# A table of 18 sets of scheduling allowances by stretch of 16 units, and attention copies from PSUM that go to ScalarE or VectorE

## The chip, the cores and the metric

One core of one Trainium2 chip. The metric is the device time of one launch in microseconds. A core has TensorE for matmuls (PE in the profile; PEld is its loading of weights), VectorE (DVE), ScalarE (ACT), GpSimd (POOL) and SyncE (SP), which here issues all DMAs. Each engine works through its own queue in order. An instruction that must wait for another engine holds up everything behind it in its own queue.

## The reference, cut to what matters

```
h   = mab(inducing, x)                    # 32 inducing points attend to 12480 tokens, 4 batches
out = mab(x, h)                           # each token attends to the 32 rows of h
# mab(q, kv): s = q @ kv.T / sqrt(128); a = softmax(s); a @ kv
x = out.reshape(49920, 128)
h = x @ w_in                              # 128 -> 2048
P = a0 + a1*h + a2*h**2 + a3*h**3
Q = 1 + |b0|*|h| + |b1|*h**2
out = (P / (Q + 1e-6)) @ w_out            # 2048 -> 128
```

## The kernel before, in words

The kernel computes a first layer and a second one around a rational function of 2048 hidden values per token. The tokens stand in 104 tiles of 480 (4 batches of 26), the hidden values in 8 groups of 256. A tile with a group is a **unit** (`b_n_q` in the names), 832 in all, 128 partitions by 960 numbers each.

A unit goes through these steps. PE multiplies into a PSUM bank pair, `h` (`first`, L964): the rows of `st` are `w_in` already multiplied by the 32 rows of `h` of that batch, so the token's softmax weights `at` are the moving operand. Of two units, the even one ("masked") gets its absolute value on DVE (`u<-h`, int32) or, when DVE is late, on ACT (event `taken`), then a shift on POOL (`pre`, `l<-u,all`) and its numerator on DVE (`D`, `l<-h,all,l`). The odd one gets its absolute value on ACT (`abs`, `u<-h,all`) and `D` (`l<-u,all,h`) on DVE. `D` frees the bank. ACT then takes the logarithm of two units at once (`ln`, `u<-u,all`, 1920 wide), and later a sigmoid, in one of three forms: into a PSUM bank for one unit (`sigp`, `i<-u`), after which DVE finishes (`Ev`, `l<-l,all,i`), or in SBUF for one unit or two (`sig`, `sig2`, `u<-u`, 960 or 1920 wide), after which POOL finishes in two instructions (`add`, `l<-l,all`, and `Eg`, `l<-l,u`). Logarithm and sigmoid need different tables, so ACT works in rounds: a table load, some logarithms, a table load, some sigmoids. There are 3 bank pairs for `h` and `i` together. Last, PE adds the unit to its tile's output, `po` (`second`, L974), DVE copies a full output to `oT` (`fetch`, L991), and SP stores it.

Beside the units run two chains of attention work, as Python generators that yield what they need next. `ahead` (L934) prepares the next batch: scores `pc`, their softmax `e`, the transpose `pt` and its copy to SBUF `eT` (`score`, L606), the weighted sum `ph` (`weigh`), then `HT`, the four pieces `pg` of `st` with their copies `gs` (`piece`, L756; two copies of 256 columns each, then a cast and a subtraction in `split`), and the linear part with `pgt` and its copy `gt` (`linear`, L802). `attend` (L948) makes the softmax weights of four tiles at a time: `pd`, `a`, a transpose `pa`, its copy `hl` (`quotients`, L878), the rest of that number on DVE into the other half of `hl`, and 16 DMAs `at<-hl` that spread it over four tiles. There is one buffer `hl`, so the next copy waits for these DMAs. All these matmul results share one PSUM bank (`misc`).

What order all this stands in is not written by hand. Class `Flow` (L188) plans the whole program ahead, while it is built. It keeps a clock per engine, a cost for every event (`COST`), and takes at each step the event that can start first. Between events of one engine that could start within the allowance `WAIT` it takes the one with the smallest sum of ready time and `RANK` (for attention work `GEN`). `LOAD` and `FULL` say how a backlog of DVE or POOL shifts the choice among the three forms of sigmoid. In the kernel before these numbers hold for the whole program. The order is then pinned: every instruction carries the semaphores it needs, and nothing is decided at run time. Which engine a copy stands on is written in the generators:

```
yield "a", 0.56                                     # eT (L643), hl (L898): ScalarE
nc.scalar.activation(eT[:, :, rows], pt[0:TP, :, rows], AF.Identity, bias=0.0, scale=1.0)
yield "v", 0.5                                      # gs (L777): VectorE, once per half
nc.vector.tensor_scalar(out=g[:, h], in0=pg[:, h], scalar1=self.scale, scalar2=None, op0=ALU.mult)
```

`gt` (L815) is on ScalarE too. Until `Flow` starts (the first 94 us, `self.boot`), the order is that of the Python program.

Of the kernel before, what the change touches and what calls it, by code (L numbers as in the profile page):

```python
# [187 lines left out]
class Flow:  # L188
# [167 lines left out]
    def do(self, what, u, start, end):  # L356
# [44 lines left out]
        elif what == "again":  # L401
            k.first(u, True)
            u.t["d"], u.moved = end + 0.1 + LAT, True
            self.pres.remove(u)
            self.ds.append(u)
# [89 lines left out]
class Kernel:  # L495
# [260 lines left out]
    def piece(self, b, j):  # L756

        nc = self.nc
        extra = j == self.F // 512
# [5 lines left out]
        if extra:  # L765
            for i, q in enumerate(qs):
                nc.tensor.matmul(pg[:, 2 * P * i:2 * P * i + 2 * P], self.HT[b], self.w_in[:, 2 * P * q:2 * P * q + 2 * P], start=True, stop=True)
        else:
            nc.tensor.matmul(pg, self.HT[b], self.w_in[:, 512 * j:512 * j + 512], start=True, stop=True)
# [382 lines left out]
```

## Time and profile before

| | |
|---|---|
| runs | 2318.00, 2318.13, 2320.06 us (median 2318.13) |
| the profiled execution | 2318.69 us, of which the span from the first to the last instruction is 2316.9 |
| granted TensorE clock, mean | 0.975 of full |
| busy, of the span | PE 2111.2, DVE 2053.4, ACT 2162.6, POOL 2009.5 us |
| units' matmuls begin | 92.98 us |
| last instruction of ACT, of DVE | begin at 2298.57 (four sigmoids, 3.65 us) and 2311.28 us |

Busy times of engines overlap, so they don't add up to the span. A row of a table by group gives the line (L165 for everything, since one helper records all instructions), engine, operation, output and inputs by the program's names, shape, count, then busy time and mean time of one, then the time for which the engine stood idle before these instructions and who ended it. A row of waits says which group of an engine waited for which of another, the sum in us, how often, and the longest.

### The profile page before, as it was taken

The page shows a single profiled execution, that of the slowest core. Times are in us where ns is not written, and L with a number is a line of the kernel's source. Part 1 is how long each engine was busy: PE and PEld are TensorE (multiplying, and loading weights), DVE is VectorE, ACT ScalarE, POOL GpSimd, SP SyncE. Part 2 cuts the span into 40 slices and gives each one's busy share as a digit, 9 for nine tenths or more (in the row PEclk, how much of TensorE's full clock was granted, in tenths as well). Part 3 has the DMA queues.
Part 4 walks back from the last instruction along what each step waited for, and adds up shares of the span by engine and source line. Part 5 has one row for each costly group of instructions (what it writes and reads, how often), then busy time and mean ns, then how long its engine had stood idle before and what let it go on. Part 6 is the DMA issues. An engine that isn't in the chain of part 4 may idle for free.

```text
span 2316.9 us, 24295 instructions
## 1 busy us (share of the span) xinstructions
PE 2111.2 (91%) x7744; PEld 1160.7 (50%) x7744; DVE 2053.4 (89%) x2204; ACT 2162.6 (93%) x1824; POOL 2009.5 (87%) x1425
## 2 busy tenths in 40 slices
PE   5689999899999999998998999999899998899888
PEld 3455555444555545454554555454455554454443
DVE  5688999989999998999999899898999998988895
ACT  1389999999999999999999999999999999999997
POOL 1269987999999896999998989999989999998995
PEclk7589999999999999999999999999999999999999
DMA  9222322211022221220121223221110111011000
GB/s 277 56 64 62 93 78 60 60 43 43 22 74 59 77 69 60 77 69 24 36 60 52 65 72 94 60 69 35 43 43 19 42 43 43 26 43 35 17 26 19
DMA packets 78639, 133.70 MB, mean 58 GB/s; under 512 B 13544, under 2 KB 63976, under 8 KB 78504
## 3 DMA queue, kind: packets, MB, share of 16 engines
q1 hardware_dynamic: 78504, 132.06, 19.4%
q8 instruction: 65, 1.06, 0.2%
q14 instruction: 70, 0.57, 0.1%
HBM read 80.89 MB, written 25.56 MB: 46 GB/s over the span
## 4 chain that ended last, share of the span: by engine, by line
ACT 25%; POOL 23%; PE 23%; DVE 16%; issue 8%; DMA 1%; SPq 1%; ACTq 0%; POOLq 0%; DVEq 0%
POOL l L165 23%; ACT u L165 18%; PE po L165 15%; DVE l L165 10%; ACT i L165 4%; PE h L165 4%; DVE u L165 3%; ACT L165 2%; PE ph L165 2%; SPq L165 1%; PE pd L165 1%; DMA at<-hl 1%; DVE oT L165 1%; DMA xT<-x_c 1%; PE pgt L165 0%
## 5 line engine op out<-in xcount | busy, mean ns | idle before, releaser
L165 PE MATMUL po<-l,w_out 128*128 128x480 f32 x3328 | 1472.1, 576 | 72.2 <-DVE oT L165 40.6
L165 POOL TENSOR_TENSOR l<-l,u 128x960 f32<-128x960 f32 x458 | 1026.7, 2242 | 37.7 <-ACT u L165 12.8
L165 PEld LDWEIGHTS po<-l,w_out 128*128 128x128 f32 x3328 | 614.7, 191 | 601.9 <-issue 457.5
L165 ACT ACTIVATE u<-u,all 128x1920 f32<-128x1920 f32 x416 | 774.3, 1892 | 4.8 <-DVE l L165 4.3
L165 PE MATMUL h<-at,st 128*128 128x480 f32 x1664 | 647.6, 482 | 81.8 <-DVE l L165 73.3
L165 POOL TENSOR_SCALAR l<-u,all 128x960 f32<-128x960 f32 x416 | 444.7, 1070 | 148.8 <-DVE u L165 121.3
L165 DVE SCALAR_TENSOR_TENSOR l<-u,all,h 128x960 f32<-128x960 f32 x416 | 501.0, 1207 | 57.4 <-ACT u L165 56.3
L165 DVE SCALAR_TENSOR_TENSOR l<-h,all,l 128x960 f32<-128x960 f32 x416 | 500.9, 1211 | 50.6 <-POOL l L165 47.8
L165 DVE TENSOR_SCALAR u<-h 128x960 int32<-128x960 int32 x400 | 457.7, 1149 | 44.2 <-PE h L165 37.1
L165 POOL TENSOR_SCALAR l<-l,all 128x960 f32<-128x960 f32 x458 | 491.0, 1072 | 1.5
L165 PEld LDWEIGHTS h<-at,st 128*128 128x128 f32 x1664 | 295.5, 192 | 384.1 <-issue 193.9
L165 DVE SCALAR_TENSOR_TENSOR l<-l,all,i 128x960 f32<-128x960 f32 x374 | 442.8, 1207 | 39.1 <-ACT i L165 38.1
L165 ACT ACTIVATE u<-h,all 128x960 f32<-128x960 f32 x416 | 435.8, 1050 | 19.8 <-PE h L165 16.2
L165 ACT ACTIVATE u<-u 128x960 f32<-128x960 f32 (+1 forms) x300 | 417.9, 1415 | 0.2
L165 ACT ACTIVATE i<-u 128x960 f32<-128x960 f32 x374 | 354.8, 965 | 16.4 <-DVE l L165 14.3
L165 ACT ACT_TABLE_LOAD x148 | 189.9, 1283 | 3.3 <-PEq L1145 0.7
L165 PEld LDWEIGHTS pd<-HT,xT 128*120 128x120 f32 x832 | 106.8, 192 | 25.1 <-issue 16.6
L165 PE MATMUL pd<-HT,xT 128*120 128x32 f32 x832 | 101.2, 267 | 5.2 <-issue 3.8
L165 PE MATMUL po<-at,st 128*128 128x480 f32 x104 | 78.1, 751 | 1.6 <-POOL st L165 1.6
L165 DVE COPY oT<-po 128x480 f32<-128x480 f32 x104 | 67.3, 647 | 12.7 <-PE po L165 12.7
L165 POOL TENSOR_TENSOR cv<-cv 128x384 f32<-128x384 f32 (+2 forms) x11 | 12.2, 1114 | 67.4 <-DVE cv L165 53.4
L165 ACT ACTIVATE e<-pc,nm 128x480 f32<-128x480 f32 (+1 forms) x28 | 18.4, 657 | 50.3 <-DVE nm L165 47.2
(96 smaller groups left out, 707.2 us busy)
## 6 DMA issues: line engine op xcount, KB each, us to landing
xT<-x_c SPq DMA_DIRECT2D x182, 240.0 KB, 3.2
x<-x_t SPq DMA_DIRECT2D x104, 240.0 KB, 4.2
at<-hl SPq DMA_DIRECT2D x416, 60.0 KB, 2.0
out<-oT SPq DMA_DIRECT2D x104, 240.0 KB, 2.2
xTw<-x_c SPq DMA_DIRECT2D x5, 960.0 KB, 10.8
raw<-w_in SPq DMA_DIRECT2D x4, 480.0 KB, 9.4
raw<-w_out SPq DMA_DIRECT2D x5, 384.0 KB, 9.7
xTw<-x_c SPq DMA_DIRECT2D x2, 480.0 KB, 8.7
```

The costliest lines, as they stand in the source:

```text
L165: ins = call(*args, **kw)
```

## The change

Three things change. The planner's numbers become 18 sets (`SETS`), of which each stretch of 16 units takes one (`PLAN`, 52 entries): before each step, `plan` looks at how many units have been added to an output and loads the set of that stretch into `RANK`, `GEN`, `WAIT`, `LOAD` and `FULL`. The copies `eT`, `gs`, `gt` and the first half of `hl` ask for "either", and the planner offers them on ScalarE with the rank `GEN["ac"]` and on VectorE with `GEN["vc"]`; the new function `copy` writes the instruction for whichever engine was taken. And a path that no unit took before (`EXTRA`, `again`) is removed; `MASKED` may differ by batch but is the same for all four. What a unit computes does not change.

```diff
-    GEN = {"pe": 110.4, "v": 80.9, "a": 9.2, "g": 75.8, "x": -14.3}
+    GEN = {"pe": 110.4, "v": 80.9, "a": 9.2, "ac": 9.2, "vc": 30.0, "g": 75.8, "x": -14.3}
+    SPAN = 16
+    KEYS = ("RANK.first", "RANK.second", "RANK.fetch", "RANK.D", "RANK.mask", "RANK.Ev", "RANK.abs", "RANK.ln", "RANK.wide", "RANK.one", "RANK.sig", "RANK.pre", "RANK.add", "RANK.Eg", "RANK.load", "RANK.take", "GEN.pe", "GEN.v", "GEN.a", "GEN.ac", "GEN.vc", "GEN.g", "GEN.x", "WAIT.pe", "WAIT.v", "WAIT.a", "WAIT.g", "LOAD.v", "LOAD.g", "FULL",)
+    SETS = (
+        (-52.7, 123.6, -33.4, 11.7, -22, 1.8, -15.1, 19.8, 56.7, 28.7, -167.4, 11.5, 86.9, 76.3, 9.6, 38, 110.4, 80.9, 9.2, 9.2, 30, 75.8, -14.3, 0.1, 0.06, 0, 0.26, -0.17, -1.05, 15),
...
+        (-51.1, 123.6, -33.4, 11.7, -22, 1.3, -15.1, 19.8, 57.9, 28.7, -155.4, 11.5, 92.3, 106.7, 9.6, 38.7, 110.4, 80.9, -7.4, 9.2, 41.8, 75.8, -12.3, 0.1, 0.06, 0, 0.2, -0.17, -1.05, 16.5),
...
+    )
+    PLAN = (16, 6, 17, 10, 7, 12, 0, 13, 0, 4, 17, 5, 9, 4, 11, 17, 6, 12, 12, 0, 3, 6, 2, 13, 11, 8, 17, 11, 6, 6, 3, 15, 14, 13, 4, 16, 6, 16, 17, 3, 12, 5, 16, 0, 2, 1, 14, 14, 4, 14, 0, 0)
...
+    def plan(self):
+        n = min(self.i2 // self.SPAN, len(self.PLAN) - 1)
+        if n == self.stretch:
+            return
+        self.stretch = n
+        for key, value in zip(self.KEYS, self.SETS[self.PLAN[n]]):
+            name, _, kind = key.partition(".")
+            if kind:
+                getattr(self, name)[kind] = value
+            else:
+                setattr(self, name, value)
...
+            elif kind == "either":
+                for engine in ("a", "v"):
+                    yield engine, t.ready, self.GEN[engine + "c"], cost, ("turn", t)
...
             ways = {}
+            self.plan()
...
+            self.by = engine
...
+    def copy(self, out, in_, scale=1.0, shift=0.0):
+        if self.flow is None or self.flow.by == "a":
+            self.nc.scalar.activation(out, in_, AF.Identity, bias=shift, scale=scale)
+        elif isinstance(scale, float) and isinstance(shift, float):
+            self.nc.vector.tensor_copy(out=out, in_=in_)
+        else:
+            self.nc.vector.tensor_scalar(out=out, in0=in_, scalar1=scale, scalar2=shift, op0=ALU.mult, op1=ALU.add)
...
-        yield "a", 0.56
-        nc.scalar.activation(eT[:, :, rows], pt[0:TP, :, rows], AF.Identity, bias=0.0, scale=1.0)
+        yield "either", 0.56
+        self.copy(eT[:, :, rows], pt[0:TP, :, rows])
...
-            moved = extra or self.shifted(q)
-            if self.boot:
-                nc.scalar.activation(g[:, h], pg[:, h], AF.Identity, bias=self.params.k2 if moved else 0.0, scale=self.scale)
-                continue
-            yield "v", 0.5
-            if moved:
-                nc.vector.tensor_scalar(out=g[:, h], in0=pg[:, h], scalar1=self.scale, scalar2=self.params.k2, op0=ALU.mult, op1=ALU.add)
-            else:
-                nc.vector.tensor_scalar(out=g[:, h], in0=pg[:, h], scalar1=self.scale, scalar2=None, op0=ALU.mult)
+            yield "either", 0.45
+            self.copy(g[:, h], pg[:, h], self.scale, self.params.k2 if self.shifted(b, q) else 0.0)
...
-        yield "a", 0.56
-        nc.scalar.activation(gt, pt[:, 0:self.NF], AF.Identity, bias=self.params.lin_shift, scale=self.params.lin_scale)
+        yield "either", 0.6
+        self.copy(gt, pt[:, 0:self.NF], self.params.lin_scale, self.params.lin_shift)
...
-        yield "a", 0.56
-        nc.scalar.activation(hl[rows, 0], pt[rows, 0:BT], AF.Identity, bias=0.0, scale=1.0)
+        yield "either", 0.56
+        self.copy(hl[rows, 0], pt[rows, 0:BT])
```

Where the orders differ, at three places. In the names `po0_0` is the output of batch 0, tile 0; `l0_0_4` unit 4 of that tile; `h0_1_0` the first product of the next tile; the last number is a buffer's.

**The start, PE's queue.** Batch 1 begins with the scores `pc1_0`, while tile 0 is still being added up. Before:

```order
L165 MATMUL po0_0_0_823<-l0_0_2_765,w_out_93 128x480 x2
L165 MATMUL po0_0_0_823<-l0_0_3_778,w_out_93 128x480 x2
L165 MATMUL pa0_1_907<-ident_76,a0_1_752 96x120 x4
L165 MATMUL po0_0_0_823<-l0_0_4_812,w_out_93 128x480 x2
L165 MATMUL po0_0_0_823<-l0_0_5_818,w_out_93 128x480 x2
L165 MATMUL pc1_0_936<-xT1_0_888,ind_74 32x480
L165 MATMUL pc1_0_936<-xT1_1_890,ind_74 32x480
L165 MATMUL pc1_0_936<-xT1_2_892,ind_74 32x480
L165 MATMUL pc1_0_936<-xT1_3_894,ind_74 32x480
L165 MATMUL h0_1_0_956<-at0_1_0_921,st_0_700 128x480 x2
```

Now:

```order
L165 MATMUL po0_0_0_828<-l0_0_2_765,w_out_93 128x480 x2
L165 MATMUL pa0_1_900<-ident_76,a0_1_752 96x120 x4
L165 MATMUL po0_0_0_828<-l0_0_3_785,w_out_93 128x480 x2
L165 MATMUL pc1_0_929<-xT1_0_869,ind_74 32x480
L165 MATMUL pc1_0_929<-xT1_1_871,ind_74 32x480
L165 MATMUL pc1_0_929<-xT1_2_873,ind_74 32x480
L165 MATMUL pc1_0_929<-xT1_3_875,ind_74 32x480
L165 MATMUL po0_0_0_828<-l0_0_4_808,w_out_93 128x480 x2
L165 MATMUL h0_1_0_953<-at0_1_0_913,st_0_700 128x480 x2
```

The scores have moved ahead of the last two pairs of tile 0's output that stood before them, and the transpose `pa0_1`, whose copy feeds tile 1, stands directly behind one pair of `po0_0` instead of two.

**The copy `hl` of batch 3, tiles 4 to 7.** On ACT before (its other half follows on DVE):

```order
L165 ACTIVATE u3_2_0_11900<-u3_2_0_11900,all_94 128x1920
L165 ACTIVATE u3_2_2_11921<-h3_2_3_11934,all_94 128x960
L165 ACT_TABLE_LOAD
L165 ACTIVATE i3_0_6_11972<-u3_0_6_11712 128x2x480
L165 ACTIVATE hl3_4_11961<-pa3_4_11956 128x480
L165 ACTIVATE i3_0_7_11979<-u3_0_6_11712 128x2x480
L165 ACTIVATE i3_1_0_11985<-u3_1_0_11737 128x2x480
```

On DVE now, with the first half as a `CAST`, and the second half as before:

```order
L165 COPY oT2_25_11956<-po2_25_0_11815 128x480
L165 TENSOR_SCALAR u3_2_4_11944<-h3_2_4_11946 128x960
L165 SCALAR_TENSOR_TENSOR l3_2_3_11921<-u3_2_2_11908,all_94,h3_2_3_11922 128x960
L165 CAST hl3_4_11955<-pa3_4_11950 128x480
L165 SCALAR_TENSOR_TENSOR l3_0_6_11711<-l3_0_6_11711,all_94,i3_0_6_11966 128x960
L165 SCALAR_TENSOR_TENSOR l3_0_7_11735<-l3_0_7_11735,all_94,i3_0_7_11972 128x960
L165 SCALAR_TENSOR_TENSOR l3_2_4_11945<-h3_2_4_11946,all_94,l3_2_4_11945 128x960
L165 TENSOR_TENSOR hl3_4_11955<-pa3_4_11950,hl3_4_11955 128x480
```

ACT's queue no longer holds this copy; DVE's now holds it, with two `Ev` (`l3_0_6`, `l3_0_7`) and one `D` between it and its second half. Counted over the program, 14 of 29 `hl`, 14 of 28 `eT` and 2 of 4 `gt` go from ACT to DVE, and 18 of 28 `gs` go from DVE to ACT. Among the units, 369 instead of 374 sigmoids go to PSUM (and so to DVE's `Ev`), 463 instead of 458 units are finished on POOL, 161 instead of 158 sigmoids are two units wide and 141 instead of 142 one unit wide in SBUF, and ACT takes the absolute value of 20 instead of 16 masked units. In the first 104 units POOL finishes 64 instead of 55, of them 6 instead of 3 in tile 0. The table loads are 148 in both, and PE's and SP's instructions are the same in number and kind.

**The end, PE's queue**, from the last but one product `h3_25_6` on. Before:

```order
L165 MATMUL h3_25_6_14714<-at3_24_1_14558,st_3_11207 128x480 x2
L165 MATMUL po3_23_0_14687<-l3_23_2_14434,w_out_93 128x480 x2
L165 MATMUL po3_23_0_14687<-l3_23_3_14455,w_out_93 128x480 x2
L165 MATMUL po3_23_0_14687<-l3_23_6_14488,w_out_93 128x480 x2
L165 MATMUL h3_25_7_14740<-at3_24_1_14558,st_3_11207 128x480 x2
L165 MATMUL po3_23_0_14687<-l3_23_5_14476,w_out_93 128x480 x2
L165 MATMUL po3_23_0_14687<-l3_23_7_14498,w_out_93 128x480 x2
L165 MATMUL po3_23_0_14687<-at3_20_3_14326,st_3_11207 128x480
L165 MATMUL po3_24_0_14759<-l3_24_0_14508,w_out_93 128x480 x2
L165 MATMUL po3_24_0_14759<-l3_24_2_14546,w_out_93 128x480 x2
```

Now:

```order
L165 MATMUL po3_23_0_14659<-l3_23_6_14485,w_out_93 128x480 x2
L165 MATMUL h3_25_5_14721<-at3_24_1_14542,st_3_11257 128x480 x2
L165 MATMUL po3_23_0_14659<-l3_23_7_14510,w_out_93 128x480 x2
L165 MATMUL po3_23_0_14659<-at3_20_3_14332,st_3_11257 128x480
L165 MATMUL h3_25_6_14735<-at3_24_1_14542,st_3_11257 128x480 x2
L165 MATMUL h3_25_7_14744<-at3_24_1_14542,st_3_11257 128x480 x2
L165 MATMUL po3_24_0_14749<-l3_24_0_14533,w_out_93 128x480 x2
L165 MATMUL po3_24_0_14749<-l3_24_1_14552,w_out_93 128x480 x2
L165 MATMUL po3_24_0_14749<-l3_24_4_14585,w_out_93 128x480 x2
```

The additions to output 23 that stood behind the last product `h3_25_7` (`l3_23_5`, `l3_23_7` and the linear part `at3_20_3`) now stand ahead of the last two. On DVE the copy of output 23, which stood behind the `D` of `l3_25_7`, now stands ahead of it. Outputs 24 and 25 follow in both.

## Rows read from the trace of the kernel before

**Rows 1.** The page, busy time, share of the span and instructions of each engine

```profile
PE 2111.2 (91%) x7744; PEld 1160.7 (50%) x7744; DVE 2053.4 (89%) x2204; ACT 2162.6 (93%) x1824; POOL 2009.5 (87%) x1425
```

**Rows 2.** The page, chain that ended last, shares by engine

```profile
ACT 25%; POOL 23%; PE 23%; DVE 16%; issue 8%; DMA 1%; SPq 1%; ACTq 0%; POOLq 0%; DVEq 0%
```

**Rows 3.** Windows: length, then busy us (instructions) of PE, PEld, DVE, ACT, POOL, clock

```profile
84.00:136.00 52.00, 42.26 (x158) 26.33 (x159) 32.99 (x42) 32.90 (x35) 15.78 (x14) 0.74 0.19 49
136.00:385.00 249.00, 233.98 (x951) 133.43 (x951) 229.45 (x232) 246.40 (x212) 219.19 (x158) 0.96 0.25 72
136.00:2302.00 2166.00, 2009.57 (x7208) 1098.88 (x7208) 1971.89 (x1962) 2117.83 (x1766) 1980.84 (x1394) 0.99 0.18 52
```

**Rows 4.** ACT's waits from 136 to 2302 us: sum, times, longest

```profile
ACT i L165 <- DVE l L165: 14.3, 26, 1.9
...
ACT u L165 <- PE h L165: 13.1, 20, 2.2
...
ACT hl L165 <- DMA at<-hl: 7.3, 6, 1.8
...
ACT hl L165 <- DMA x<-x_t: 1.7, 2, 1.3
...
ACT hl L165 <- PE h L165: 1.3, 1, 1.3
```

**Rows 5.** Timeline of ACT: two `hl` that waited for DMAs

```profile
315.93 0.57 ACT L165 ACTIVATE hl<-pa 128x480 fp32r<-128x480 f32 x1 [0.45 <-DMA x<-x_t]
...
1797.95 0.57 ACT L165 ACTIVATE hl<-pa 128x480 fp32r<-128x480 f32 x1 [1.26 <-DMA at<-hl]
```

**Rows 6.** ACT by group and shape: busy us, mean ns, idle before

```profile
L165 ACT ACTIVATE eT<-pt 120x512 f32<-120x512 f32 x24 | 14.3, 594 | 7.4 <-PE pt L165 7.4
...
L165 ACT ACTIVATE hl<-pa 128x480 fp32r<-128x480 f32 x23 | 13.0, 565 | 8.7 <-DMA at<-hl 6.8 <-DMA x<-x_t 1.7
...
L165 ACT ACTIVATE gs<-pg,all 128x256 f32<-128x256 f32 x4 | 1.9, 516 | 1.8 <-PE pg L165 1.8
...
L165 ACT ACTIVATE i<-u 128x960 f32<-128x960 f32 x374 | 354.8, 965 | 16.4 <-DVE l L165 14.3 <-PE po L165 0.7 <-PE h L165 0.2
...
L165 ACT ACTIVATE u<-h 128x960 f32<-128x960 f32 x16 | 15.4, 962 | 3.3 <-PE h L165 3.3
...
L165 ACT ACTIVATE u<-u 128x1920 f32<-128x1920 f32 x158 | 281.9, 1796 | 0.2
```

**Rows 7.** DVE by group and shape

```profile
L165 DVE COPY oT<-po 128x480 f32<-128x480 f32 x104 | 67.3, 647 | 12.7 <-PE po L165 12.7
...
L165 DVE TENSOR_SCALAR gs<-pg,all 128x256 f32<-128x256 f32 x28 | 13.6, 498 | 0.1
...
L165 DVE SCALAR_TENSOR_TENSOR l<-l,all,i 128x960 f32<-128x960 f32 x374 | 442.8, 1207 | 39.1 <-ACT i L165 38.1
...
L165 DVE TENSOR_SCALAR u<-h 128x960 int32<-128x960 int32 x400 | 457.7, 1149 | 44.2 <-PE h L165 37.1 <-POOL l L165 6.2
```

**Rows 8.** POOL by group and shape

```profile
L165 POOL TENSOR_TENSOR l<-l,u 128x960 f32<-128x960 f32 x458 | 1026.7, 2242 | 37.7 <-ACT u L165 12.8
...
L165 POOL TENSOR_SCALAR l<-l,all 128x960 f32<-128x960 f32 x458 | 491.0, 1072 | 1.5
```

**Rows 9.** ACT's waits from 84 to 136 us

```profile
ACT e L165 <- DVE nm L165: 4.5, 1, 4.5
```

**Rows 10.** The chain that ended last, 84 to 140 us: start, length, what

```profile
124.40 3.23 PE po L165 x8
```

**Rows 11.** Timeline of the end: start, length, group, idle before, releaser

```profile
2298.57 3.65 ACT L165 ACTIVATE i<-u 128x960 f32<-128x960 f32 x4
...
2299.57 4.59 DVE L165 SCALAR_TENSOR_TENSOR l<-l,all,i 128x960 f32<-128x960 f32 x4 [1.75 <-ACT i L165]
...
2283.77 13.15 PE L165 MATMUL po<-l,w_out 128*128 128x480 f32 x32 [1.70 <-DVE oT L165]
...
2297.88 13.15 PE L165 MATMUL po<-l,w_out 128*128 128x480 f32 x32 [0.75 <-DVE oT L165]
```

More of the change, by code (lines that the diff above doesn't have):

```diff
@@ L191 @@
     LAT = 0.15
-    COST = {"first": 0.56, "second": 1.60, "linear": 0.35, "again": 0.6, "fetch": 0.6, "D": 1.13, "mask": 1.08, "Ev": 1.13, "abs": 0.95, "ln": 1.79, "sig": 1.70, "half": 0.90, "load": 1.4, "pre": 1.06, "add": 1.11, "Eg": 2.22}
-    RANK = {"again": 40, "first": -52.7, "second": 123.6, "fetch": -33.4, "D": 11.7, "mask": -22, "Ev": 1.8, "abs": -15.1, "ln": 19.8, "wide": 56.7, "one": 28.7, "sig": -167.4, "pre": 11.5, "add": 86.9, "Eg": 76.3, "load": 9.6, "take": 38}
+    COST = {"first": 0.56, "second": 1.60, "linear": 0.35, "fetch": 0.6, "D": 1.13, "mask": 1.08, "Ev": 1.13, "abs": 0.95, "ln": 1.79, "sig": 1.70, "half": 0.90, "load": 1.4, "pre": 1.06, "add": 1.11, "Eg": 2.22}
+    RANK = {"first": -52.7, "second": 123.6, "fetch": -33.4, "D": 11.7, "mask": -22, "Ev": 1.8, "abs": -15.1, "ln": 19.8, "wide": 56.7, "one": 28.7, "sig": -167.4, "pre": 11.5, "add": 86.9, "Eg": 76.3, "load": 9.6, "take": 38}
     LOAD = {"v": -0.17, "g": -1.05}
-    GEN = {"pe": 110.4, "v": 80.9, "a": 9.2, "g": 75.8, "x": -14.3}
+    GEN = {"pe": 110.4, "v": 80.9, "a": 9.2, "ac": 9.2, "vc": 30.0, "g": 75.8, "x": -14.3}
     WAIT = {"pe": 0.1, "v": 0.06, "a": 0, "g": 0.26}
+    SPAN = 16
+    KEYS = ("RANK.first", "RANK.second", "RANK.fetch", "RANK.D", "RANK.mask", "RANK.Ev", "RANK.abs", "RANK.ln", "RANK.wide", "RANK.one", "RANK.sig", "RANK.pre", "RANK.add", "RANK.Eg", "RANK.load", "RANK.take", "GEN.pe", "GEN.v", "GEN.a", "GEN.ac", "GEN.vc", "GEN.g", "GEN.x", "WAIT.pe", "WAIT.v", "WAIT.a", "WAIT.g", "LOAD.v", "LOAD.g", "FULL",)
+    SETS = (
[18 rows of a table added]
+    )
+    PLAN = (16, 6, 17, 10, 7, 12, 0, 13, 0, 4, 17, 5, 9, 4, 11, 17, 6, 12, 12, 0, 3, 6, 2, 13, 11, 8, 17, 11, 6, 6, 3, 15, 14, 13, 4, 16, 6, 16, 17, 3, 12, 5, 16, 0, 2, 1, 14, 14, 4, 14, 0, 0)
     BATCH = 6
@@ L205 @@
     FULL = 15.0
-    MASKED = (0, 2, 4, 6)
-    EXTRA = ()
+    MASKED = ((0, 2, 4, 6),) * 4
     def __init__(self, k, units):
         self.k, self.units = k, units
+        self.RANK, self.LOAD, self.GEN, self.WAIT = dict(self.RANK), dict(self.LOAD), dict(self.GEN), dict(self.WAIT)
+        self.stretch = -1
         self.T = dict.fromkeys(("pe", "v", "a", "g"), 0.0)
@@ L400, in do @@
             self.pres.append(u)
[L401 to L405, printed above, removed]
         elif what == "pre":
@@ L416, in do @@
         elif what == "D":
-            if u.masked and not u.moved:
+            if u.masked:
                 V.scalar_tensor_tensor(out=u.g, in0=u.h, scalar=p.k2, in1=u.g, op0=ALU.add, op1=ALU.mult)
@@ L764, in piece @@
         pg = self.misc(f"pg{b}_{j}")
[L765 to L769 removed]
+        nc.tensor.matmul(pg, self.HT[b], self.w_in[:, 512 * j:512 * j + 512], start=True, stop=True)
         g = self.ap.tile([P, 512], F32, tag="gs", name=f"gs{b}_{j}", bufs=2)
@@ L930, in opening @@
         yield from self.linear(0)
-        if Flow.EXTRA:
-            yield from self.piece(0, self.F // 512)
     def ahead(self):
@@ L944, in ahead @@
             yield from self.linear(b)
-            if Flow.EXTRA:
-                yield from self.piece(b, self.F // 512)
     def groups(self, first):
@@ L955, in attend, with shifted, first @@
             yield from self.tokens(b, self.groups(0), lambda n: self.reach(b, n - 9))
-    def shifted(self, q):
-        return self.fast and q not in Flow.MASKED
+    def shifted(self, b, q):
+        return self.fast and q not in Flow.MASKED[b % len(Flow.MASKED)]
     def hp(self, u, name):
         return self.ps_h.tile([P, 2, 512], F32, tag=f"hp{u.bank}", name=f"{name}{u.i}", bufs=1)[:, :, 0:BT]
-    def first(self, u, again=False):
+    def first(self, u):
         nc = self.nc
@@ L970, in first @@
         for k in range(2):
-            f = P * (2 * (Flow.EXTRA.index(q) if again else q) + k)
-            nc.tensor.matmul(u.h[:, k], (self.sx if again else self.st[b])[:, f:f + P], u.rhs, start=True, stop=True)
+            f = P * (2 * q + k)
+            nc.tensor.matmul(u.h[:, k], self.st[b][:, f:f + P], u.rhs, start=True, stop=True)
     def second(self, u, done=None):
```

13 lines of the change are left out of this document (3 added, 10 removed), and 16 rows, old and new, of the table SETS.

## The prediction

> **What bounds the kernel now.** I read the busy times of the page first. ScalarE leads with 2162.6 us of a span of 2316.9, but PE, DVE and POOL follow at 87 to 91% [rows 1]. An average hides the start, so I looked at windows next. Before 136 us nothing is full: from 84 to 136 us ACT works 32.90 of 52 us and POOL 15.78. From 136 to 2302 us ACT works 2117.83 of 2166 us, 97.8%, and DVE 1971.89, 91.0% [rows 3]. In that stretch ACT is nearly a solid line, and the time can only fall by less work on ACT or fewer gaps in it. The third view is what these gaps wait for. The longest sums are 14.3 us for DVE to free a PSUM bank for a sigmoid, 13.1 us for PE's next product, and 10.3 us (7.3, 1.7 and 1.3) in front of the copy `hl` [rows 4]. The last view, the chain of waits, gives a warning: only 25% of it lies on ACT, 23% each on POOL and PE, 16% on DVE [rows 2]. The four are loaded so evenly that the chain hops among them.
>
> The sum below is made against the profiled execution, 2318.69 us. The median of the runs shown, 2318.13, lies 0.56 us under it.
>
> **Term 1, the work on ACT.** From ACT go 14 `eT` at 0.594 us, 14 `hl` at 0.565, 2 `gt` as wide as `eT`, 5 sigmoids into PSUM at 0.965 and one of the same width in SBUF: 8.3 + 7.9 + 1.2 + 4.8 + 1.0 = 23.2 us. To it come 18 `gs` at 0.516, 4 absolute values at 0.962 and 3 wide sigmoids at 1.796: 9.3 + 3.8 + 5.4 = 18.5 us [rows 6]. Three of the `eT` are half as wide and cost less than that row, so I take 4.5 us less instead of 4.7. The table loads stay 148. On a solid engine this counts in full.
>
> **Term 2, the gaps in front of `hl`.** There is one buffer `hl`, so the copy waits until the 16 DMAs of the copy before have read it. Nine of the 29 copies wait on ACT, 10.3 us in sum [rows 4]. The copies that go to DVE hold five of these waits: I followed the 29 copies by name in both orders and in the timeline, and the five waited 0.45 to 1.33 us, 5.6 us of the 10.3 (the first and the last of them are [rows 5]). These waits don't vanish. They now stand in DVE's queue, with `Ev` and `D` behind them, as in the second place of the order. DVE is idle for 2166 - 1972 = 194 us of this stretch [rows 3], and that is the cover. If it is gone, ACT waits the same time for a bank, and the term is zero. Ends: 0 and -10.3. I take -5.6, since DVE's idle time is 35 times the wait.
>
> **What DVE and POOL get for it.** DVE takes 14 `hl` and 14 `eT`. The nearest row is its copy of an output from PSUM, 128x480 in 0.647 us, so `hl` is 14 x 0.65 = 9.1 us and the slightly wider `eT` and `gt` 16 x 0.69 = 11.0. It loses 18 `gs` at 0.498, 5 `Ev` at 1.207 and 4 masks at 1.149, 9.0 + 6.0 + 4.6 = 19.6 us [rows 7]. That leaves DVE 0.5 us more, nothing of 1972. POOL gets 5 more units at 2.242 + 1.072 = 3.31 us, 16.6 us in all [rows 8], on 1980.84 of 2166 [rows 3], and goes from 91.5 to 92.2%. It is not the fullest engine with that, and I cost it at nothing over the whole. Where it comes in one piece it is a rival below. PE and SP keep all their instructions. On SP loads and stores only change places a few times; a load that comes late would show in the 1.7 us that `hl` waits for `x<-x_t` [rows 4], and I cost that at nothing too.
>
> **Term 3, the gaps for banks.** The new sets re-cut the order of all units, and here lie 27.4 us of ACT's gaps (14.3 and 13.1) [rows 4]. There are still three bank pairs, and their users change by 5 sigmoids in 1206 (832 products and 374 sigmoids). No count says that the gaps should shrink or grow, and the trace of before can't show an order that it didn't run. Ends: -27.4, all of it, and +27.4, as much again. I take 0, which is where the counts point, and keep half of each end for the rivals.
>
> **Term 4, the start.** In the old order the scores of batch 1 stand on PE behind two more pairs of the output of tile 0, and these 8 matmuls took 3.23 us [rows 10]. ACT, waiting for the softmax of these scores, stood still for 4.5 us [rows 9]. In the new order the scores stand ahead of both, and the transpose that feeds tile 1 comes one pair (half of 3.23, 1.6 us) earlier. The gain can't be more than the wait of 4.5, and the first product of tile 1 still needs its DMAs. Against it, POOL finishes three more units in tile 0, 3 x 3.31 = 9.9 us in a stretch where it has 52 - 15.8 = 36 us free [rows 3]; the cover is there, but a late one could hold `po0_0` and the scores behind it. Ends: -4.5 and +3.3 (one such unit). I take -2, near the 1.6 us of the pair.
>
> **Term 5, the end.** ACT's last four sigmoids begin at 2298.57 and take 3.65 us. DVE's last four `Ev` end at 2299.57 + 4.59 = 2304.16. PE however works off outputs 24 and 25 in two runs of 13.15 us, each of 8 units of 1.64, and the second begins only at 2297.88 [rows 11]. So PE, not ACT, sets the end. In the new order two units and the linear part of output 23 (about 3.6 us) have moved ahead of the last two products, and on DVE the copy of output 23 no longer stands behind the last `D`, for which PE had waited 1.70 us [rows 11]. Output 24 can begin up to 5 us earlier. Then the `Ev` become the limit: the first of the last four is done at 2300.8, four units of 1.64 follow, and PE ends near 2307.8 where it ended at 2311.2. Ends: -3.5 and 0. I take -3.
>
> **Sum.** -4.5 - 5.6 + 0 - 2 - 3 = -15.1, so 2318.69 - 15.1 = 2303.6, and 0.56 less for the median: 2303.
>
> **Weighing a rule.** Terms 1 and 2 count every microsecond taken from ACT in full, because ACT is the fullest engine [rows 3]. The chain [rows 2] says that a microsecond on ACT is on the path a quarter of the time. The Trainium skill, Perfetto Trace Analysis, section Identifying the Most-Contended Engine, takes the side of the first: for engines other than TensorE the occupancy names the bottleneck, and that engine is to be improved first. By it terms 1 and 2 are 10.1 us, by the chain 2.5. I go with the windows, since over 2166 us an engine at 97.8% has only 48 us to give, wherever the chain hops; the chain's reading is the second rival.
>
> **Rivals.**
> *The bank gaps go too.* If the sets were well chosen for each stretch, half of the 27.4 us vanish: 2303 - 13.7 = 2289. For it: these gaps are many and short (46 gaps), which is what an order can mend. Against it: the counts don't change.
> *ACT is only one of four.* A gain on ACT turns into a wait for POOL or PE. Terms 1 and 2 shrink to 2.5 us: 2318.1 - 2.5 - 5 = 2310.6 with start and end, 2315.6 without. For it: the chain's shares, and POOL at over 91%. Against it: ACT's few gaps.
> *The bank gaps grow by as much:* 2303 + 13.7 = 2316.7.
> *POOL paces the first stretch (slower).* In the first 104 units POOL finishes nine more units, six of them after tile 0: 6 x 3.31 = 19.9 us. From 136 to 385 us it works 219.19 of 249, with 29.8 idle [rows 3]. If that idle time is waiting that the new order can't fill, the stretch grows by 19.9 us, and 2303 + 19.9 = 2323. It decides from the point at which more than 15.1 of the 19.9 us are not covered. Against it: 239 of 249 still fits, and DVE, for whose masks POOL waits, loses nine `Ev` there.
> *That the copies stay where they were* is excluded by the order: 30 are on DVE's queue and 18 on ACT's.
>
> **How the numbers follow.** A measurement of this kernel can tell about 0.2%, 4.6 us. The forecast (2297 to 2309) has 0.48, the bank gaps gone 0.16, ACT as one of four 0.24 (0.14 with start and end, 0.10 without), the bank gaps grown 0.04, POOL 0.08. Faster: 0.48 + 0.16 + 0.14 = 0.78. Same: 0.10 + 0.04 = 0.14. Slower: 0.08. The range from 2291 to 2317 leaves out POOL's case and about half of the second, 0.16.
>
> **What would show it.** In the changed profile ACT's busy time falls by 4 to 5 us and DVE's stays. The waits of `hl` on ACT fall to about 5 us, and DVE shows the others. The scores of batch 1 come before 127 us, and the second run of 32 matmuls begins 3 to 5 us nearer to ACT's last sigmoids. I am wrong if ACT's bank gaps move by more than 10 us either way, if POOL's busy share from 136 to 385 us passes ACT's, or if ACT loses work and its idle time grows by as much.

## The result, and the profile after

The changed kernel takes 2296.72 us (median of 4 runs, 2295.69 to 2298.41), the kernel before 2318.07 us beside it. The ratio is 0.9905, 95% interval 0.9892 to 0.9917: faster by 0.95%, 21.4 us. The forecast was 2303, in a range of 2291 to 2317.

The profiled execution took 2295.76 us, 22.9 less than that of before. Two lines of its page, busy time by engine and the chain's shares, answer to [rows 1, 2]:

```profile
PE 2109.9 (92%) x7744; PEld 1153.3 (50%) x7744; DVE 2046.9 (89%) x2207; ACT 2158.2 (94%) x1813; POOL 2026.1 (88%) x1435
...
ACT 32%; POOL 28%; PE 16%; DVE 12%; issue 8%; DMA 2%; SPq 0%; ACTq 0%; POOLq 0%; DVEq 0%
```

ACT lost 4.4 us of work, DVE 6.5, and POOL gained 16.6. PE's busy time (1.3 us less) and its mean granted clock (0.975 in both) are what they were. Windows of the changed kernel, with the columns of [rows 3]; everything here stands 8 us earlier at the start and 19 us earlier at the end:

```profile
84.00:128.00 44.00, 37.17 (x147) 21.98 (x146) 27.44 (x34) 33.08 (x35) 25.71 (x20) 0.79 0.21 54
128.00:377.00 249.00, 230.19 (x911) 128.91 (x910) 229.56 (x232) 243.43 (x198) 231.79 (x166) 0.97 0.24 72
128.00:2283.00 2155.00, 2016.28 (x7226) 1097.66 (x7225) 1970.18 (x1970) 2113.12 (x1754) 1987.48 (x1398) 0.99 0.18 52
```

ACT does the work of the start in 44 us instead of 52. The long stretch is 11 us shorter, of which ACT's work is 4.7. What ACT waited for in it, to be laid beside [rows 4]:

```profile
ACT i L165 <- DVE l L165: 14.9, 22, 3.4
ACT u L165 <- PE h L165: 12.4, 16, 2.1
ACT u L165 <- DVE l L165: 3.9, 4, 1.7
ACT hl L165 <- DMA at<-hl: 3.8, 2, 2.3
ACT u L165 <- POOL l L165: 0.5, 2, 0.3
```

The two sums for banks are what they were, 27.3 us against 27.4. The waits in front of `hl` fell from 10.3 to 3.8 us. For the start, ACT's waits from 84 to 128 us [rows 9]:

```profile
ACT u L165 <- PE h L165: 6.5, 3, 3.2
ACT gs L165 <- PE pg L165: 3.2, 3, 1.4
ACT e L165 <- DVE nm L165: 1.4, 1, 1.4
```

Last the timeline: the scores of batch 1 on PE and their softmax `e` on ACT, then the end [rows 10, 11]:

```profile
118.18 1.01 PE L165 MATMUL pc<-xT,ind 128*32 128x480 f32 x8
...
120.28 0.66 ACT L165 ACTIVATE e<-pc,nm 128x480 f32<-128x480 f32 x1 [1.37 <-DVE nm L165]
...
2260.45 13.15 PE L165 MATMUL po<-l,w_out 128*128 128x480 f32 x32
...
2274.97 13.43 PE L165 MATMUL po<-l,w_out 128*128 128x480 f32 x32 [1.15 <-DVE oT L165]
...
2279.41 3.65 ACT L165 ACTIVATE i<-u 128x960 f32<-128x960 f32 x4
```

The second run of 32 products now begins 4.44 us ahead of ACT's last four sigmoids, where it was 0.69. From these sigmoids to the end of the span it is 14.5 us instead of 18.3.

The span can be cut at three points on ACT: its first absolute value of a unit, the table load that follows the softmax of batch 1's first scores, and its last four sigmoids. Between the second and the third the time is ACT's busy time plus its idle time, with nothing left over. All runs of this study in these pieces, from windows and timelines of the profiled executions, in us:

| kernel | before the first | start | long stretch: ACT busy + idle | end | waits for PE's `h`, 136 to 2250 | PE busy, all |
|---|---|---|---|---|---|---|
| before | 94.2 | 45.6 | 2110.6 + 48.2 | 18.3 | 13.1 | 2111.2 |
| changed | 92.3 | 39.5 | 2105.8 + 41.9 | 14.5 | 12.4 | 2109.9 |
| e1 copies only | 92.1 | 41.6 | 2119.8 + 78.2 | 21.5 | 36.0 | 2133.8 |
| e2 sets only | 92.2 | 47.3 | 2122.9 + 90.3 | 17.0 | 40.8 | 2142.0 |
| e3 copies home | 92.3 | 42.4 | 2114.7 + 48.3 | 14.5 | 16.9 | 2120.6 |
| e4 `hl` home | 91.4 | 41.6 | 2112.3 + 44.6 | 14.5 | 12.9 | 2119.4 |
| e5 sets rotated | 91.9 | 39.5 | 2108.0 + 71.6 | 22.7 | 31.1 | 2123.6 |
| e6 before, two buffers | 92.1 | 46.0 | 2111.4 + 40.9 | 18.0 | 13.1 | 2109.3 |
| e7 changed, two buffers | 92.3 | 39.8 | 2106.0 + 39.7 | 14.5 | 12.7 | 2114.4 |
| e8 `hl` home, two buffers | 91.9 | 40.0 | 2111.7 + 37.3 | 14.4 | 12.4 | 2108.6 |
| e9 36 copies more on ACT | 91.9 | 39.6 | 2124.0 + 47.6 | 14.5 | 16.7 | 2125.5 |
| e10 the same on DVE | 94.4 | 40.2 | 2108.4 + 58.9 | 14.4 | 20.2 | 2119.6 |
| e11 the same on POOL | 95.1 | 39.6 | 2108.4 + 48.9 | 14.5 | 17.0 | 2113.5 |
| e12 before, another set | 92.5 | 45.6 | 2121.2 + 67.4 | 21.5 | 32.4 | 2121.9 |

So the 22.9 us are 1.9 before the first point, 6.1 in the start, 4.8 of ACT's work, 6.3 of its gaps and 3.8 at the end. The 1.9 are not the change's: that part of the program is the same in all these kernels, and its length varied from 91.4 to 95.1 us.

### The profile page after: what moved, and what is told of

Its sections match the earlier page's. It is cut to its first block, busy times and chain, and to the rows that moved or that the text cites. A ratio compares the mean times of both kernels' runs of the same rounds, so it can differ in the third digit from the quotient of the medians.

```text
span 2294.0 us, 24207 instructions
## 1 busy us (share of the span) xinstructions
PE 2109.9 (92%) x7744; PEld 1153.3 (50%) x7744; DVE 2046.9 (89%) x2207; ACT 2158.2 (94%) x1813; POOL 2026.1 (88%) x1435
## 4 chain that ended last, share of the span: by engine, by line
ACT 32%; POOL 28%; PE 16%; DVE 12%; issue 8%; DMA 2%; SPq 0%; ACTq 0%; POOLq 0%; DVEq 0%
POOL l L165 28%; ACT u L165 23%; PE po L165 10%; DVE l L165 7%; ACT i L165 6%; PE h L165 3%; ACT L165 3%; DVE u L165 3%; DMA x<-x_t 1%; PE ph L165 1%; DVE oT L165 0%; DMA raw<-w_out 0%; SPq L165 0%; PE pd L165 0%; PE pg L165 0%
## 5 line engine op out<-in xcount | busy, mean ns | idle before, releaser
L165 POOL TENSOR_TENSOR l<-l,u 128x960 f32<-128x960 f32 x463 | 1038.0, 2242 | 46.6 <-ACT u L165 19.8
L165 PE MATMUL h<-at,st 128*128 128x480 f32 x1664 | 633.5, 475 | 83.5 <-DVE l L165 75.1
L165 POOL TENSOR_SCALAR l<-l,all 128x960 f32<-128x960 f32 x463 | 496.0, 1071 | 1.5
L165 DVE SCALAR_TENSOR_TENSOR l<-l,all,i 128x960 f32<-128x960 f32 x369 | 437.1, 1208 | 42.0 <-ACT i L165 41.0
L165 ACT ACTIVATE u<-u 128x1920 f32<-128x1920 f32 (+1 forms) x302 | 422.0, 1421 | 0.2
L165 ACT ACTIVATE i<-u 128x960 f32<-128x960 f32 x369 | 349.9, 965 | 17.1 <-DVE l L165 14.9
```

The lines of the kernel that those rows point to most:

```text
L165: ins = call(*args, **kw)
```

## Experiments

**Which part brings the gain.** In e1 every stretch takes the old numbers (set 0), and the copies keep their choice. In e2 the sets stay and the copies are pinned where they were.

```diff
-    PLAN = (16, 6, 17, 10, 7, ...)
+    PLAN = (0, 0, 0, 0, 0, ...)          # e1
-        yield "either", 0.56
+        yield "a", 0.56                  # e2: eT, hl, gt; gs gets "v"
```

e1. 

> The copies may go to either engine, but one set of numbers (the old one) holds for the whole program. Against the kernel before, ScalarE loses 7 eT, 10 hl and 2 gt and gains 18 gs, 5 sigmoids into PSUM, 4 wide sigmoids and 11 absolute values, and loses 13 sigmoids of one unit: about +7.7 us of work. The order of the start is that of the changed kernel, the order of the end that of before. Theory (ScalarE's work and gaps count in full, start and end apart): 2318 + 7.7 - 8 (start) - 3 (gaps of hl) = about 2315. Rival, a microsecond on ScalarE is worth a quarter: 2318 + 1.9 - 8 - 1 = 2311. Rival, the copies are the gain and the sets nothing: 2297.

e2. 

> The 18 sets stay, the copies are pinned where they were before (eT, hl, gt on ScalarE, gs on VectorE). Against the kernel before, ScalarE gains 9 sigmoids of one unit and 9 absolute values and loses 5 sigmoids into PSUM and 2 wide ones: about +9.2 us of work. The order of the start is that of before, the end has output 23 ahead of the last two products as in the changed kernel. Theory: 2318 + 9.2 - 3 (end) = 2324. Rival, a quarter: 2318 + 2.3 - 3 = 2317. Rival, the sets are the gain and the copies nothing: 2297 to 2300.

Measured: e1 2353.2 us, ratio to before 1.0142 (1.0126 to 1.0157); e2 2370.4 us, 1.0214 (1.0200 to 1.0228). Each half alone makes the kernel slower, by 34 and 51 us, and every expectation missed by 30 or more. The first rows of ACT's waits from 136 to 2250 us, of e1 and then of e2:

```profile
ACT u L165 <- PE h L165: 36.0, 33, 6.7
ACT i L165 <- DVE l L165: 15.8, 26, 3.0
ACT hl L165 <- DMA at<-hl: 8.9, 7, 1.7
```

```profile
ACT u L165 <- PE h L165: 40.8, 44, 5.5
ACT i L165 <- DVE l L165: 13.0, 27, 2.5
ACT u L165 <- DVE l L165: 9.0, 11, 2.0
```

ACT's added work was as counted, within about 3 us. What was not in any sum are 23 and 28 us more of waiting for PE's products. The start does split: with the freedom of the copies and the old numbers it takes 41.6 us (e1), with the sets alone 47.3 (e2), with both 39.5. But in e1 every engine's instructions stand in the changed kernel's order until after the start, so the 2.0 us between these two are not the sets' (term 4 below).

**Is the order fitted?** e5 gives the same sets to other stretches; e12 gives the kernel before one neighbouring set.

```diff
-    PLAN = (16, 6, 17, 10, ... 8, 17, 11, ...)
+    PLAN = (16, 6, 11, 6, 6, 3, ... 17, 10, ... 17)   # e5: turned by 25 places
+    PLAN = (1,) * 52                                   # e12, with the copies pinned
```

e5. 

> The changed kernel with the same sets, but from the third stretch on each stretch takes the set of another (the list of sets is turned by 25 places). Against the kernel before ScalarE loses 13 eT, 19 hl, 2 gt and 13 sigmoids into PSUM and gains 18 gs, 6 wide sigmoids, 1 of one unit and 5 absolute values: about -6.5 us of work. Theory of the counts (work, gaps of hl, start; bank gaps unchanged): 2318 - 6.5 - 5 - 6 = 2300. Rival (each set is fitted to what its stretch happens to meet, and any other order loses gaps for PE's products): 2340 to 2370, as with the copies alone or the sets alone, and 15 us or more of added waits of ScalarE for PE's h.

e12. 

> The kernel before (copies pinned as there) with another of the 18 sets for the whole program; it differs from the old numbers in 6 of 30, by 0.3 to 10. ScalarE gets 18 more sigmoids of one unit, 9 fewer wide ones and 9 more absolute values, about 17.9 - 16.2 + 8.7 = +10.4 us of work. If the old numbers were an ordinary point and only the counts matter: 2319 + 10 x (a quarter to all) = 2322 to 2329. If the order of the kernel before is itself a fitted one, and any neighbour loses gaps for PE's products: 2335 or more, with ScalarE's waits for h at 25 us or more instead of 13.1.

Measured: e5 2331.8 us, 1.0046 (1.0029 to 1.0064); e12 2349.2 us, 1.0115 (1.0091 to 1.0139). Both counts failed, and the waits for `h` rose to 31.1 and 32.4 us as the second theory had it, though e5 lost less than its 2340. In e12 the sigmoids into PSUM are 374, as before, so the number of users of the banks did not change at all. So the order of the kernel before is no ordinary one either, since the one neighbour that was tried (e12) loses 31 us. The four other orders tried (e1, e2, e5, e12) all lost, 13 to 51 us at medians. Four are few, and how the sets were found is not on record; that the two good orders are fitted to what their units meet is an inference from these losses.

One place can be followed. It is the longest wait of ACT for `h` in e1, 6.72 us. Timeline of e1 around it:

```profile
262.73 0.66 ACT L165 ACTIVATE e<-pc,nm 128x480 f32<-128x480 f32 x1
...
264.97 0.57 PE L165 MATMUL pa<-ident,a 120*128 120x120 f32 x4
...
267.74 0.65 DVE L165 CAST hl<-pa 128x480 fp32r<-128x480 f32 x1
...
270.54 6.71 PE L165 MATMUL po<-l,w_out 128*128 128x480 f32 x16 [0.31 <-DVE oT L165]
...
279.16 1.84 PE L165 MATMUL h<-at,st 128*128 128x480 f32 x6
...
280.17 0.97 ACT L165 ACTIVATE u<-h 128x960 f32<-128x960 f32 x1 [6.72 <-PE h L165]
...
281.04 1.16 DVE L165 TENSOR_SCALAR u<-h 128x960 int32<-128x960 int32 x1 [9.96 <-PE h L165]
```

This `hl` is that of tiles 8 to 11 of batch 0, and the products need what its DMAs spread. In the kernel before the same copy began at 234.24 us, in the changed one at 237.41, in e1 at 267.74, in e5 at 256.86 and in e12 at 271.25. What differs is PE's order. `pa0_8`, its transpose, and `pc1_2`, the next scores of batch 1, share the bank `misc`. The kernel before and the changed one give it to `pa0_8` first; e1, e5 and e12 give it to `pc1_2` first:

```
before, changed:  pa0_4  pc1_1  pd0_8  pt1_1  ph1_1  pa0_8
e1, e5, e12:      pa0_4  pc1_1  pd0_8  pt1_1  ph1_1  pc1_2  pa0_8
```

`pc1_2` keeps the bank until its softmax `e` has read it. That began at 262.73 us in e1, at 251.4 in e5 and at 265.0 in e12, and `pa0_8` followed at 264.97, 254.8 and 266.2. The longest wait of e5 (7.04 us, at 272.67) and of e12 (5.96, at 283.61) is the same place. That of e2 (5.52, at 936.00) follows a late `hl` too, `hl1_12` at 924.98, with its first product at 935.28. But there the bank is taken in the same order as in the kernel before, where that `hl` came at 873.01 without such a wait behind it, so scores ahead of a transpose are not harmful by themselves, and the cause in e2 stays open. No run swaps the two back and leaves the rest.

The late weights are only the first half of it. The four DMAs of tile 8 had landed by 272.26 us in e1, before ACT ran dry at 273.45, and its product began 6.9 us after them. It stood in PE's queue behind the 16 additions to outputs shown above, some `pd` and four more additions. In e5 the weights landed at 265.59 and the product began at 271.66, in e12 at 278.68 and 282.90, in e2 at 931.57 and 935.28, each time behind such additions. That the planner put these ahead because it counted on late weights is likely, but not shown. Meanwhile ACT, DVE and POOL all run dry, with PE busy. Two windows of e1, with the columns of [rows 3]:

```profile
274.00:277.00 3.00, 3.00 (x9) 1.37 (x8) 0.00 (x0) 0.00 (x0) 0.36 (x1) 1.00 0.31 102
...
292.00:295.00 3.00, 3.00 (x36) 2.55 (x28) 3.00 (x4) 3.00 (x3) 2.58 (x3) 0.50 0.18 35
```

The second shows an after-effect: PE, which had then waited itself (0.98 us busy from 286 to 289), was granted half its clock, its lower level of 1.2 GHz. The same 7744 matmuls kept PE busy 23.9 us longer in e1 and 32.1 in e2 than in the changed kernel. One such place is a wait of 6 to 7 us, in losses of 13 to 51. The rest is spread over many short waits (33 in e1 and 44 in e2 with the long ones) whose places I did not follow.

**The gaps of `hl`, and which engine copies.** With the order kept, e4 writes the 14 moved `hl` on ACT again, and e3 all 48 moved copies where they were.

```diff
-        self.copy(hl[rows, 0], pt[rows, 0:BT])
+        self.copy(hl[rows, 0], pt[rows, 0:BT], by="a")   # e4; e3: eT, gt too, and gs by="v"
```

e3. 

> The order of the changed kernel, but each of its 48 moved copies is written on the engine it had before, at the same place in the program. ScalarE gets 14 x 0.594 + 14 x 0.565 + 2 x 0.766 = 17.8 us and loses 18 x 0.523 = 9.4 us, so +8.4 us, and the waits of hl that now stand on VectorE (5.5 us) come back to it. Theory, in full: 2296.7 + 8.4 + 5.5 = 2311. Rival, a quarter: 2300. Rival, the gain is the order of the units and the engine of a copy is worth nothing: 2297.

e4. 

> The order of the changed kernel, but the 14 hl on VectorE are written on ScalarE, at the same place in the program. ScalarE gets 14 x 0.565 = 7.9 us and 5.5 us of waits; VectorE loses 14 x 0.654 = 9.2 us and the same waits. Theory, in full: 2296.7 + 13.4 = 2310. If only the work counts and the waits are hidden: 2304.6. Rival, a quarter: 2300. Worth nothing: 2297.

Measured: e3 2313.0 us, 0.9976 (0.9966 to 0.9985); e4 2307.7 us, 0.9951 (0.9938 to 0.9965). Both fit the theory that ACT's time counts in full, e4 between its two forms. But e4 mixes work and waits. So e6 (the kernel before), e7 (the changed one) and e8 (e4) get two buffers for the first half of `hl` and one for the second, with the order as it was:

```diff
-        hl = ap.tile([P, 2, BT], F32R, tag="hl", name=f"hl{b}_{n0}")
+        hi = ap.tile([P, BT], F32R, tag="hi", name=f"hi{b}_{n0}", bufs=2)
+        lo = ap.tile([P, BT], F32R, tag="lo", name=f"lo{b}_{n0}")
```

e6. 

> The kernel before, but the first half of hl has two buffers and the second half one of its own, so that ScalarE's copy no longer waits for the 16 DMAs of the copy before; the order is the same, and the subtraction on VectorE takes over the wait. Theory (gaps on ScalarE count in full, VectorE's idle time covers the wait): -7.3 us, 2311 to 2312 beside a before of about 2319. Rival, a quarter of it: 2317. Rival, the gap only moves to VectorE and comes back as a bank gap: no change.

e7. 

> The changed kernel with the same two buffers. Two gaps of ScalarE for these DMAs are left there, 3.8 us in sum. Theory, in full: 2296.7 - 3.8 = 2293. Rival, a quarter: 2295.8. Rival, the fitted order is upset and it gets slower: above 2298.

e8. 

> The changed kernel with its 14 moved hl back on ScalarE, and the two buffers. Beside the same without the buffers (2307.7, waits of hl for the DMAs 5.5 us and for x 2.3 us) it shows how much of those 11 us was the waits. Theory: the waits go and the work of 7.9 us stays, 2296.7 + 7.9 - 3.8 = 2301 to 2302. Rival, the waits cost nothing: 2307.7.

Measured: e6 2310.9 us, 0.9969 (0.9958 to 0.9980); e7 2294.75 us, 0.9895 (0.9875 to 0.9914); e8 2296.7 us, 0.9901 (0.9883 to 0.9920). ACT's waits of e6 from 136 to 2250 us, where [rows 4] had three rows of `hl`:

```profile
ACT i L165 <- DVE l L165: 17.9, 31, 1.9
ACT u L165 <- PE h L165: 13.1, 20, 2.2
ACT u L165 <- DVE l L165: 2.3, 5, 1.1
ACT e L165 <- DVE nm L165: 1.2, 1, 1.2
```

All waits of `hl` are gone, 10.3 us. 3.6 came back as waits of `i` for a bank, and the time fell by 7.2 us by the ratio, 7.9 by the medians. The gaps of one buffer were real time, and a third of the whole gain was to be had without any new order. e8 against e4 is the same queue but for the buffers, and gives 11 us, which is the 7.8 us of waits within an uncertainty of about 5. It brings e8 back to the changed kernel's median. And e8 against e7, 14 copies on ACT or on DVE with no such wait on ACT in either, differ by 2.0 us at medians (0.0006 in the ratio, inside both intervals), though ACT works 5.9 us more. So these runs show no difference by which engine makes the copy; four of each are too few to exclude one of some 5 us. What stood in ACT's queue behind the wait was worth much. e7 is not told apart from the changed kernel by these runs.

**The price of a microsecond.** The changed kernel with 36 extra copies, one beside every third output, on one engine; nobody waits for them, and the planner does not know of them.

```diff
         self.full = None
+        if self.flow is not None and n % 3 == 0:
+            self.nc.scalar.activation(self.spare, self.w_in[:, 0:480], AF.Identity, bias=0.0, scale=1.0)   # e9; vector e10, gpsimd e11
         return True
```

e9. 

> The changed kernel with 36 extra copies on ScalarE (128x480, from weights into a tile that nobody reads), one beside every third output; nothing waits for them. At about 0.57 us each (as hl) that is 20.5 us more work on ScalarE, in the same order. If a microsecond of ScalarE's work counts in full: 2296.7 + 20.5 = 2317. If a quarter, as its share of the chain and as the 14 hl of the run with two buffers (2.0 us for 7.9 us) say: 2302. If nothing: 2297.

e10. 

> The same 36 copies on VectorE, between 0.3 and 0.65 us each, 11 to 23 us more work there. By my terms (VectorE's idle time covers it): 2297 to 2298. By VectorE's share of the chain, an eighth: 2298 to 2300. In full: 2308 to 2320.

e11. 

> The same 36 copies on GpSimd, about 0.55 us each (half of 1.07 for 960 columns), 20 us more work there. By my terms: 2297. By GpSimd's share of the chain, 28 in 100: 2302. In full: 2317.

Measured: e9 2317.15 us, 0.9985 (0.9973 to 0.9997); e10 2321.45 us, 1.0006 (0.9994 to 1.0019); e11 2308.5 us, 0.9948 (0.9931 to 0.9966). The group of the extra copies in each, ACT, DVE, POOL (busy us, mean ns):

```profile
L165 ACT ACTIVATE spare<-w_in 128x480 f32<-128x480 f32 x36 | 21.4, 595 | 0.1
```

```profile
L165 DVE TENSOR_SCALAR spare<-w_in 128x480 f32<-128x480 f32 x36 | 34.3, 954 | 0.0
```

```profile
L165 POOL TENSOR_SCALAR spare<-w_in 128x480 f32<-128x480 f32 x36 | 21.5, 597 | 0.1
```

By the ratios, against 0.9905 of the changed kernel, the time rose by 0.0080, 0.0101 and 0.0043 of 2318: 18.5, 23.4 and 10.0 us, each with an uncertainty of 4 to 5 (the two intervals together). Per microsecond of the group that is 0.9 on ACT, 0.7 on DVE and 0.5 on POOL, give or take 0.2. ACT's added work counts in full within the uncertainty. Nor is DVE's and POOL's free: 11 and 12% of idle time do not cover work that comes at a place the order has not made room for. In e10 ACT's idle time in the long stretch rose from 41.9 to 58.9 us. But the 0.7 is no price of DVE's work as such. More than half of the 34.3 us is standing still beside POOL (last section), since such a copy can take 0.40 us, 14.4 for all 36, and POOL's busy time rose by 7.3 us with them. So the three numbers do not rank the engines.

## Why the prediction was right, and where not

**The sum.** The range held, and the sum was 5.9 us short: 15.1 forecast, 21.0 measured in the same pieces (4.8 of work, 6.3 of gaps, 6.1 at the start, 3.8 at the end), beside the 1.9 that are not the change's. The median of 2296.72 lies just under the forecast's own band (2297 to 2309), where I had expected to land only if the bank gaps went; they did not, and most of the shortfall is term 4.

**Term 1** had the size right: ACT's work fell by 4.8 us in the long stretch where I had 4.5 (`gt` is 0.766 us there, not 0.594 as I took it). Its price in full is shown for work added on ACT alone (e9); for a copy that leaves ACT for DVE, as here, it is not shown (e8 against e7). Wrong was the step beside it, "I cost it at nothing", for POOL. By e11, 16.6 us more on POOL cost about 8, give or take 4, where no order makes room for them. e10 shows that DVE's idle time is no cover for extra work either, but not at what price. That the sum came out all the same I can only argue: the new order found the room.

**Term 2** was right, and e6 shows it by itself: 7.2 to 7.9 us for 10.3 us of gaps taken off ACT. In the change 6.5 us of them went, where I had 5.6, and DVE now waits for DMAs in front of `hl`, 6.8 us from 128 to 2283:

```profile
DVE hl L165 <- DMA at<-hl: 3.6, 4, 1.6
DVE hl L165 <- DMA x<-x_t: 2.5, 1, 2.5
...
DVE hl L165 <- DMA out<-oT: 0.7, 1, 0.7
```

The cause is the wait's place in the queue more than the work of the copy (e8). Whether DVE's idle time was a cover everywhere is open. Behind the longest of these waits stand in DVE's queue two `D` and the `Ev` that frees a bank, and ACT then waited longer than anywhere else in the long stretch. First DVE, then ACT, in the changed kernel:

```profile
772.48 0.66 DVE L165 CAST hl<-pa 128x480 fp32r<-128x480 f32 x1 [2.50 <-DMA x<-x_t]
...
778.08 1.21 DVE L165 SCALAR_TENSOR_TENSOR l<-l,all,i 128x960 f32<-128x960 f32 x1
...
779.38 0.98 ACT L165 ACTIVATE i<-u 128x960 f32<-128x960 f32 x1 [3.43 <-DVE l L165]
```

How much of the 3.43 us is the moved wait no run shows.

**Term 3** was right by its number and wrong by its reason. The gaps for banks are 27.3 us instead of 27.4. But "No count says that the gaps should shrink or grow" is no ground for a zero: in e12 that count did not change either, and the waits for `h` rose by 19 us. So as far as the prediction goes the zero was luck. That the old order and the new one are both fitted would explain it, and is not shown. In the four other orders tried the error had one sign: ACT's idle time in the long stretch was 19 to 42 us above that of the kernel before, more than any term. I gave such growth 4 in 100 and named no place for it. The one place that the runs showed is no bank of `h` and `i`, which the term counts, but the shared bank `misc`, and behind it PE's queue: in e1 the product came late because its tiles' softmax weights did, and then stood behind other work of PE.

**Term 4** was too small: 6.1 us against 2. The step that failed is "The gain can't be more than the wait of 4.5". ACT stood still 12.7 us between its first absolute value and the table load, seven waits in sum, and 6.1 in the changed kernel. The wait for the softmax of the scores, the only one I had counted, fell by 3.1 (4.5 to 1.4). A wait of 2.8 us for POOL at 98.94 us went as well: ACT now fills that place with two `gs`, which had been DVE's. That choice of engine is the smaller part, since e3, with these `gs` back on DVE in the same order, still takes 42.4 us. Nor are the sets needed for this order: e1 has it with the old numbers, and takes 41.6. What lies between e1 and the changed kernel is PE's clock. One window of the changed kernel, then the same of e1, with the columns of [rows 3]:

```profile
95.00:103.00 8.00, 6.92 (x33) 5.29 (x32) 7.37 (x9) 7.38 (x8) 3.67 (x4) 0.71 0.34 93
```

```profile
95.00:103.00 8.00, 6.92 (x29) 6.29 (x29) 5.43 (x7) 6.44 (x7) 3.35 (x3) 0.50 0.22 62
```

PE is as long busy and gets less done: all of the window in e1 lies at the lower level of the clock (0.50), part of it in the changed kernel at the full one. In the same eight us after their first absolute value e3 and e4 had 0.50 too, and starts of 42.4 and 41.6 us; e5 and e7 to e11, with the same order, 0.70 to 0.71 and 39.5 to 40.2. The old order took 45.6 us at 0.71 and 46.0 in e6 at 0.50. So the order of the start is worth about 4 us where the clock rises late and 6 where it rises early, and of the 6.1 some 2 hang on that. Why it rose when it did was not followed.

**Term 5** was right: 3.8 against 3, a little past its end of 3.5. Output 24 began 14.8 us ahead of the last sigmoids before and 18.96 now, 4.2 earlier, where I had up to 5. e3, e4 and e7 to e11, which share the order, all end within 14.4 to 14.5 us.

**The rule weighed.** For work added on ACT e9 decides for full price, against the chain's quarter: 18.5 us for 21.4 us of copies, where a quarter would be 5.4. By the Trainium skill, Perfetto Trace Analysis, section Identifying the Most-Contended Engine, the fullest engine is to be improved first. ACT's price of 0.9 fits that; that it is the dearest is not shown, since DVE's number is mixed with POOL's. The chain's shares (32, 12 and 28%) are not these prices.

**The signs I had named.** ACT's busy time (4.4 less), the waits of `hl` (3.8 left), the scores (118.2 us) and the second run (3.75 us nearer) came as said. DVE's busy time did not stay, it fell by 6.5 us; 5.9 of that are 14 casts whose count is the same (below). None of the three things that would have proved me wrong came.

## What to carry to other kernels

Where four engines are 87 to 94% full and the order is pinned, look first for a wait that stands at the head of the fullest engine's queue: a second buffer took a third of this gain, with the order as it was. Do not price a new order at nothing because its counts are the same: the four others tried here all lost, by more than any single term. Find which shared buffer feeds the next batch of work: where its copy came 23 to 37 us late (e1, e5, e12), ACT, DVE and POOL ran dry together. To learn what work on an engine costs, add some that nobody waits for and run it: the share of idle time does not tell. Choose it so that it does not meet another engine at the memory, as the DVE copies here did. And before a few microseconds of a start are put down to a change, compare PE's granted clock there.

## What the runs showed of the chip

In these runs a DVE copy from SBUF to SBUF stood still while POOL worked, and one from PSUM did not. Timeline of e10, two of the 36 copies and what POOL did beside the second:

```profile
774.60 0.40 DVE L165 TENSOR_SCALAR spare<-w_in 128x480 f32<-128x480 f32 x1
...
1639.53 2.32 DVE L165 TENSOR_SCALAR spare<-w_in 128x480 f32<-128x480 f32 x1
...
1639.35 2.24 POOL L165 TENSOR_TENSOR l<-l,u 128x960 f32<-128x960 f32 x1 [3.89 <-ACT u L165]
```

At 774.60 POOL was between two instructions, and the copy took 0.40 us. At 1639.53 POOL had just begun, and the copy ended 0.26 us after POOL's instruction, at 1641.85. So 36 copies took 954 ns in the mean instead of 400. Copies `hl` from PSUM stayed within 640 to 658 ns in the changed kernel, whatever POOL did. This agrees with the Trainium skill, SBUF — State Buffer, section Who interferes with whom: DVE's copies in a two-port mode and GpSimd exclude each other for a whole instruction. In which mode these copies ran no run here shows.

It also explains DVE's lost work. The casts `st<-gs` read SBUF and write SBUF; their group before and after:

```profile
L165 DVE TENSOR_SCALAR st<-gs 128x512 fp32r<-128x512 f32 x14 | 15.0, 1069 | 0.2
```

```profile
L165 DVE TENSOR_SCALAR st<-gs 128x512 fp32r<-128x512 f32 x14 | 9.1, 648 | 0.0
```

Their shortest is 421 ns before and 409 after; their longest fell from 2292, about the length of POOL's longest step (2242 in the mean), to 1512. The new order let them meet POOL less often. Whether that is luck or the fit of the sets was not tried.
